# LSH attention and two dense layers on one core: k and q of a head prepared in one joint tile, with SBUF-to-SBUF moves and the bucket rows on GpSimd

## Chip, core and metric

The kernel runs on one core of a Trainium2 chip. The metric is device microseconds of one execution; the time before is the median of three runs, 738.44 us (738.31 to 738.90).

## What is computed

```python
q_bits = (einsum('bhsd,dk->bhsk', q, proj) > 0)      # 6 bits; k_bits alike
mask = q_bucket[:, :, :, None] == k_bucket[:, :, None, :]
scores = where(mask, q @ k.T / 8, -1e9)
attn = softmax(scores);  x = attn @ v                # 2 x 8 heads, 768 tokens, 64 wide
h = max(x @ w1, x @ w2, x @ w3);  y = h @ w_out      # 1536 x 512 -> 768 -> 512
g = where(u >= 1, u, where(u <= -1, 0, (u + 1)**2 / 4))   # u = y @ w_in, 2048 wide
out = g @ w_out2
```

All of it is float32. A product is done on TensorE in the F32R type, each operand split in a high part (rounded to F32R) and a low part (the rest), with the product of the two low parts left out.

## The kernel before

**Attention** works on 16 heads of 768 tokens, each as 6 tiles of 128 queries: 96 tiles. Per tile TensorE makes the scores (`t_qk`, L367 and L368, four matmuls of 384 columns), VectorE takes the row extreme and copies them out of PSUM (`t_max`, L375), ScalarE exponentiates (`t_exp`, L387), TensorE transposes six 128-column blocks (`t_tr`, L395), ScalarE copies the high part out (`t_hi`, L409) and VectorE subtracts the low part (`t_lo`, L413); every three tiles twelve value matmuls follow (`g_pv`, L421), then a correction on ScalarE (`g_corr`) and an addition on VectorE (`g_add`, L440). Every two heads the row sums are inverted, stored to DRAM and loaded back spread over partitions (`pair_*`, L447 to L466), and `norm_*` writes `x_hl` (L475 to L488).

**A head's preparation** runs one to two heads ahead. k and q come from DRAM already transposed, each twice over (rows 0 to 63 and again 64 to 127), in two tiles `kr` and `qr` (`load_one`, L274). GpSimd scales q (L300), makes the high parts `ak` and `aq` of both copies (L293), and subtracts the low parts of 64 rows: of k into `bk` rows 0 to 63, of q into `aq` rows 64 to 127 (`prep_lo`, L318, two halves each). Two SBUF-to-SBUF DMAs copy the high part of q into `bq` rows 0 to 63 and `bk` rows 64 to 127 (`prep_dup`, L305). TensorE multiplies with the split projection (`bits_mm`, L337, three matmuls a half), ScalarE takes the sign (`bits_sign`, L344), and `bits_row` (L354) turns the signs into 12 extra rows at rows 64 to 75, so that the second score matmul (76 rows) adds the mask: the row for `bk` on VectorE, the row for `bq` on GpSimd. Head 0 is prepared ahead of the loop on ScalarE and VectorE.

**The order** of the loop comes from a planner in the program (`Work`, L42 to L94): tasks with an engine, a cost, a due number (in tiles), predecessors and buffers; on each engine it takes, among the tasks that could start within 0.15 us of the earliest, the one due first, and emits them in that order. Every engine and each DMA queue then runs its list strictly in order, with semaphore waits. All DMAs but one are issued on SP. The planner also puts the splitting of the first four weight slices (`w_tick`, `w_steps`, L170 to L203) into the loop.

**The dense layers** (`mlp`, L680 on) follow. Their first matmul blocks (`early`, L732) need batch 0 alone and cover the normalisation of the last two heads, which TensorE would otherwise wait for.

The words that a sentence can't say:

```python
o = s_ps[n % 2][:, half, 0:HALF]
nc.tensor.matmul(out=o, lhsT=hd["aq"][:, qs], rhs=hd["ak"][:, ks], start=True, stop=False)
nc.tensor.matmul(out=o, lhsT=hd["bq"][0:76, qs], rhs=hd["bk"][0:76, ks], start=False, stop=True)
```

Of the kernel before, what the change touches and what calls it, by code (L numbers as in the profile page):

```python
# [41 lines left out]
class Work:  # L42
# [3 lines left out]
    HOP = 0.15  # L46

# [50 lines left out]
def lsh_attention_moe_kernel(  # L98
    ctx: ExitStack,
    tc: tile.TileContext,  # L100
    q: bass.AP,
    k: bass.AP,
# [25 lines left out]
    pj_raw = const.tile([128, 2, 108], F32, name="pj_raw")  # L128
    pj_st = const.tile([128, 3, 108], F32R, name="pj_st")
# [107 lines left out]
    def attention(mlp_steps):  # L237
        with ExitStack() as ax, ExitStack() as sx:
            raw_p = ax.enter_context(tc.tile_pool(name="raw", bufs=1))
# [32 lines left out]
            def load_one(h, side):  # L272
                r = raw_p.tile([128, S], F32, tag=side + "r", name=side + "r")
                nc.sync.dma_start(out=r, in_=(k if side == "k" else q)[h])  # L274
                head.setdefault(h, {})[side + "r"] = r

            def pj_split():
                for i in range(2):
                    nc.scalar.copy(out=pj_st[:, i, :], in_=pj_raw[:, i, :])
                nc.scalar.copy(out=pj_st[0:64, 2, :], in_=pj_raw[0:64, 1, :])  # L280
                for side, i in ((0, 2), (1, 1)):
                    nc.vector.tensor_tensor(
                        out=pj_st[64:128, i, :], in0=pj_raw[64:128, side, :],
                        in1=f32(pj_st[64:128, side, :]), op=ALU.subtract,
                    )

            def prep_hi(h, side, eng, cs=slice(0, S)):
                hd = head[h]
                if "a" + side not in hd:
                    hd["a" + side] = prep_p.tile([128, S], F32R, tag="a" + side, name="a" + side)  # L290
# [596 lines left out]
```

## Time and profile before

| what | value |
|---|---|
| median of three runs | 738.44 us |
| the profiled execution, its own time | 736.59 us |
| its span, first to last instruction | 734.8 us |
| mean granted TensorE clock | 0.993 of full |
| TensorE matmuls busy | 708.8 us (96%) |
| TensorE weight loads busy | 595.7 us (81%) |
| VectorE busy | 553.7 us (75%) |
| ScalarE busy | 405.4 us (55%) |
| GpSimd busy | 348.3 us (47%) |

Busy shares of the whole span mix two parts with different limits, so the stretches have to be read apart. Matmuls are pipelined and the ends of their rows are modelled: starts tell more than lengths. In the rows PE is TensorE's matmuls, PEld its weight loads, DVE VectorE, ACT ScalarE, POOL GpSimd, SP the queue that issues DMAs; Lnn is a line of the kernel before.

### The profile page before, as it was taken

The numbers are of one execution on the slowest core, as the hardware profiler recorded it, in microseconds if no ns is written. First come the engines' busy times: TensorE is split into PE (matmuls) and PEld (weight loads), VectorE is DVE, ScalarE is ACT, GpSimd is POOL, SyncE is SP. The second block draws the span as 40 slices with busy tenths as digits, with TensorE's granted clock in tenths as the row PEclk, the third lists the DMA queues.
The fourth block names the chain that finished last, engine by engine and source line by source line (L and its number), as shares of the span: only waits on it lengthen the run. The fifth ranks groups of instructions, "written<-read, shape, count | busy, mean of one in ns | idle before, by whom it ended". The sixth has DMA issues, their size and how long they took to land.

```text
span 734.8 us, 10243 instructions
## 1 busy us (share of the span) xinstructions
PE 708.8 (96%) x3526; PEld 595.7 (81%) x3526; DVE 553.7 (75%) x898; ACT 405.4 (55%) x789; POOL 348.3 (47%) x338
## 2 busy tenths in 40 slices
PE   8899999999988999999999999999999999999998
PEld 6788888878877888888888888888888888888886
DVE  5899999999999864777544436675687888888854
ACT  5798998988988842333222223467445445444430
POOL 3779689787885301344223312253433443434430
PEclk7999999999999999999999999999999999999999
DMA  4445434534431021222211112112012211112104
GB/s 131 126 119 154 131 85 107 150 98 109 120 110 33 23 65 44 86 87 87 65 50 44 43 58 86 58 58 86 30 58 67 76 57 58 59 57 84 32 0 172
DMA packets 21668, 58.17 MB, mean 79 GB/s; under 512 B 2832, under 2 KB 6000, under 8 KB 21616
## 3 DMA queue, kind: packets, MB, share of 16 engines
q1 hardware_dynamic: 21584, 57.51, 26.2%
q8 instruction: 28, 0.46, 0.2%
q14 instruction: 24, 0.20, 0.1%
q0 software_dynamic: 32, 0.00, 0.0%
HBM read 48.41 MB, written 3.19 MB: 70 GB/s over the span
## 4 chain that ended last, share of the span: by engine, by line
PE 79%; DVE 14%; ACT 2%; issue 2%; DMA 1%; POOL 1%; SPq 0%; ACTq 0%; DVEq 0%
PE b L675 45%; PE b L802 18%; PE u_ps L421 5%; DVE pl L413 5%; PE t_ps L395 5%; DVE p L375 5%; PE s_ps L367 3%; PE s_ps L368 2%; DVE bk L354 2%; DVE u L440 1%; PE pj_ps L337 1%; ACT ph L409 1%; DMA kr<-in_k 1%; ACT z L344 1%; DMA qr<-in_q 1%
## 5 line engine op out<-in xcount | busy, mean ns | idle before, releaser
L675 PE MATMUL b<-x_hl,w 128*128 128x512 f32 (+1 forms) x900 | 202.8, 382 | 0.0
L675 PEld LDWEIGHTS b<-x_hl,w 128*128 128x128 f32 x900 | 164.0, 188 | 33.5
L702 POOL TENSOR_TENSOR g<-r,g 128x512 fp32r<-128x512 f32 x48 | 62.7, 1308 | 125.3 <-ACT g L701 125.3
L802 PE MATMUL b<-w,g 128*128 128x512 f32 (+1 forms) x438 | 108.4, 391 | 0.0
L413 DVE TENSOR_TENSOR pl<-t_ps,ph 128x384 fp32r<-128x384 f32 x192 | 97.9, 550 | 8.1 <-ACT ph L409 6.0
L207 POOL TENSOR_TENSOR w<-wg,w 128x512 fp32r<-128x512 f32 (+1 forms) x42 | 58.9, 1404 | 92.8 <-ACT w L201 80.7
L802 PEld LDWEIGHTS b<-w,g 128*128 128x128 f32 x438 | 81.8, 188 | 18.8
L375 DVE TENSOR_SCALAR_CACHE_REDUCE p<-s_ps 128x768 f32<-128x768 f32 x96 | 90.4, 948 | 7.5 <-PE t_ps L395 4.5
L409 ACT CAST ph<-t_ps 128x384 fp32r<-128x384 f32 x192 | 84.8, 481 | 20.1 <-PE t_ps L395 18.9
L387 ACT ACTIVATE p<-p,nm 128x768 f32<-128x768 f32 x96 | 90.3, 941 | 9.2 <-DVE p L375 8.2
L395 PE MATMUL t_ps<-ident,p 128*128 128x128 f32 x576 | 85.3, 280 | 9.4 <-DVE pl L413 8.8
L180 DVE SCALAR_TENSOR_TENSOR wg<-wg,wr 128x512 f32<-128x512 f32 (+1 forms) x58 | 66.9, 1154 | 34.6 <-ACT wg L178 33.8
L201 ACT CAST w<-wg 128x512 fp32r<-128x512 f32 (+1 forms) x42 | 25.4, 605 | 111.0 <-DVE wg L193 111.0
L395 PEld LDWEIGHTS t_ps<-ident,p 128*128 128x128 f32 x576 | 66.2, 141 | 24.8 <-DVE pl L413 19.2
L675 PE MATMUL b<-x_hl,wx 128*128 128x512 f32 x360 | 86.1, 395 | 0.0
L675 PEld LDWEIGHTS b<-x_hl,wx 128*128 128x128 f32 x360 | 67.8, 188 | 15.8
L367 PE MATMUL s_ps<-ak,aq 128*128 128x384 f32 x192 | 72.1, 375 | 7.9 <-DVE p L375 7.5
L782 DVE SCALAR_TENSOR_TENSOR r<-r,b 128x512 f32<-128x512 f32 x48 | 33.0, 687 | 48.6 <-ACT r L781 48.2
L368 PE MATMUL s_ps<-bk,bq 76*128 76x384 f32 x192 | 67.2, 350 | 0.0
L809 DVE TENSOR_TENSOR acc<-b,acc 128x512 f32<-128x512 f32 (+1 forms) x85 | 56.4, 675 | 8.0 <-PE b L802 8.0
L780 ACT ACTIVATE r<-b,half_sb 128x512 f32<-128x512 f32 x48 | 33.0, 687 | 46.1 <-PE b L675 38.3
L185 DVE TENSOR_SCALAR wg<-wg 128x512 int32<-128x512 int32 (+1 forms) x58 | 53.2, 917 | 2.5
(86 smaller groups left out, 1064.7 us busy)
## 6 DMA issues: line engine op xcount, KB each, us to landing
wr<-in_w SPq DMA_DIRECT2D x50, 512.0 KB, 3.4
kr<-in_k SPq DMA_DIRECT2D x15, 384.0 KB, 3.1
qr<-in_q SPq DMA_DIRECT2D x15, 384.0 KB, 3.1
vr<-in_v SPq DMA_DIRECT2D x16, 192.0 KB, 2.6
rb<-d SPq DMA_DIRECT2D x16, 192.0 KB, 3.9
wr<-in_w SPq DMA_DIRECT2D x8, 384.0 KB, 3.1
bk<-aq SPq DMA_DIRECT2D x15, 192.0 KB, 2.6
bq<-aq SPq DMA_DIRECT2D x15, 192.0 KB, 3.0
```

The costliest lines, as they stand in the source:

```text
L180: nc.vector.scalar_tensor_tensor(out=f32(g), in0=f32(g), scalar=TINY_SQ, in1=f32(high), op0=ALU.is_ge, op1=ALU.mult)
L207: nc.gpsimd.tensor_tensor(out=w[:, 1, 0:cols], in0=f32(g2), in1=f32(w[:, 0, 0:cols]), op=ALU.subtract)
L367: nc.tensor.matmul(out=o, lhsT=hd["aq"][:, qs], rhs=hd["ak"][:, ks], start=True, stop=False)
L368: nc.tensor.matmul(out=o, lhsT=hd["bq"][0:76, qs], rhs=hd["bk"][0:76, ks], start=False, stop=True)
L375: nc.vector.tensor_scalar(out=p.rearrange("p (a k) -> p a k", a=2), in0=s_ps[n % 2][:, :, 0:HALF], scalar1=MASKED, scalar2=MASKED, op0=ALU ...
L387: nc.scalar.activation(out=p, in_=p, func=ACTF.Exp, scale=-1.0, bias=tl[n]["nm"], accum_out=pair[h // 2]["sums"][:, c:c + 1],)
L395: nc.tensor.transpose(out=t_ps[half][:, j * 128:(j + 1) * 128], in_=tl[n]["p"][:, kt * 128:(kt + 1) * 128], identity=ident,)
L409: nc.scalar.copy(out=hi, in_=src)
L413: nc.vector.tensor_tensor(out=lo, in0=src, in1=f32(hi), op=ALU.subtract)
L675: nc.tensor.matmul(out=outp, lhsT=w_[a], rhs=x_[b_], start=(i == 0 and jj == 0), stop=(i == n - 1 and jj == 2),)
L702: nc.gpsimd.tensor_tensor(out=dst[:, 1, cs], in0=src, in1=f32(dst[:, 0, cs]), op=ALU.subtract)
L802: nc.tensor.matmul(out=pb[:, cs], lhsT=gs[f][:, a, tsl], rhs=wt[:, b_, cs], start=(n == 0), stop=(n == len(terms) - 1),)
```

## The change

k and q of a head come in one array `kq` and one tile `r`: k in rows 0 to 63, q in 64 to 127. GpSimd scales the q half, makes one high part `hi` and one low part `lo` (two halves of 384 columns, 128 rows). Five SBUF-to-SBUF DMAs then lay out the operands of the scores: the high part of q to `qa` and `qb` rows 0 to 63, the low part of q to `qa` rows 64 to 127, and, once the bit matmuls have read them, the high part of k over the low part of q in `lo` (`kh`) and the k bit row over q's in `hi` (`kb`). The bit rows of both sides are made by one GpSimd instruction a half over rows 64 to 108 of `qb` (`bits_rows`). The first score matmul is `qa` with `lo`, the second `qb` with `hi`. The projection tile is split in one copy and one subtraction.

Beside that: two raw tiles in place of one of each side; the planner's patience is 0.3 us on ScalarE and VectorE, several costs are changed, the bit tasks of a head are due four tiles earlier, the first two weight slices are loaded at the loop's start; and two of the eight early blocks of the dense layers move behind the others, with one buffer less for their sums.

```diff
-                    task = min((k for t, k in ready if t <= first + 0.15), key=lambda k: k["due"])
+                    task = min((k for t, k in ready if t <= first + self.PATIENCE[eng]), key=lambda k: k["due"])
...
+    PATIENCE = dict(PE=0.15, ACT=0.3, DVE=0.3, POOL=0.15, SP=0.15)
...
-            raw_p = ax.enter_context(tc.tile_pool(name="raw", bufs=1))
+            raw_p = ax.enter_context(tc.tile_pool(name="raw", bufs=2))
...
+            def prep_hi(h, copy, cs=slice(0, S)):
                 hd = head[h]
+                if "hi" not in hd:
+                    for x in ("hi", "lo", "qa", "qb"):
+                        hd[x] = prep_p.tile([128, S], F32R, tag=x, name=x)
+                copy(out=hd["hi"][:, cs], in_=hd["r"][:, cs])
+
+            def prep_lo(h, half, eng):
+                hd = head[h]
+                cs = slice(half * HALF, (half + 1) * HALF)
+                eng.tensor_tensor(out=hd["lo"][:, cs], in0=hd["r"][:, cs], in1=f32(hd["hi"][:, cs]), op=ALU.subtract)
+
+            UP, DOWN = slice(0, 64), slice(64, 128)
+            MOVES = dict(
+                qa=("qa", UP, "hi", DOWN), qb=("qb", UP, "hi", DOWN), ql=("qa", DOWN, "lo", DOWN),
+                kh=("lo", DOWN, "hi", UP), kb=("hi", slice(64, 76), "qb", slice(96, 108)),
+            )
...
-                rows = slice(96, 108) if side == "k" else slice(64, 76)
+                rows = slice(64, 108)
                 eng.tensor_scalar(
-                    out=head[h]["b" + side][64:76, cs], in0=z[rows], scalar1=pc_sb[rows, 0:1],
+                    out=head[h]["qb"][rows, cs], in0=z[rows], scalar1=pc_sb[rows, 0:1],
...
-                    nc.tensor.matmul(out=o, lhsT=hd["aq"][:, qs], rhs=hd["ak"][:, ks], start=True, stop=False)
+                    nc.tensor.matmul(out=o, lhsT=hd["qa"][:, qs], rhs=hd["lo"][:, ks], start=True, stop=False)
                     nc.tensor.matmul(
-                        out=o, lhsT=hd["bq"][0:76, qs], rhs=hd["bk"][0:76, ks], start=False, stop=True
+                        out=o, lhsT=hd["qb"][0:76, qs], rhs=hd["hi"][0:76, ks], start=False, stop=True
                     )
...
             for half in range(2):
                 cs = slice(half * HALF, (half + 1) * HALF)
                 prep_scale(0, nc.scalar, cs)
+                prep_hi(0, nc.scalar.copy, cs)
+                prep_lo(0, half, nc.vector)
                 if half == 0:
                     pj_split()
                 bits_mm(0, half, banks0[half])
+                prep_move(0, "qa", nc.vector.tensor_copy, cs)
+                prep_move(0, "ql", nc.vector.tensor_copy, cs)
+                prep_move(0, "qb", nc.gpsimd.tensor_copy, cs)
+                prep_move(0, "kh", nc.gpsimd.tensor_copy, cs)
                 bits_sign(0, half, banks0[half])
+                bits_rows(0, half, nc.vector)
+                prep_move(0, "kb", nc.vector.tensor_copy, cs)
...
+                sc = task("POOL", 0.9, due, prep_scale, h, nc.gpsimd, after=[ld])
+                hi = task("POOL", 0.8, due, prep_hi, h, nc.gpsimd.tensor_copy, after=[sc], takes=[hp], leaves=[rp])
+                lo = [task("POOL", 1.0, due, prep_lo, h, half, nc.gpsimd, after=[hi], leaves=[rp]) for half in range(2)]
+                for x, after in (("qa", [hi]), ("qb", [hi]), ("ql", lo)):
+                    move[x] = task("SP", 0.1, due, prep_move, h, x, after=after, lag=3.0)
...
-                    done.append(task("DVE", 0.35, due + 6, bits_row, h, half, "k", nc.vector, after=[sg], leaves=[zp]))
-                    done.append(task("POOL", 0.93, due + 6, bits_row, h, half, "q", nc.gpsimd, after=[sg], leaves=[zp]))
+                    mms.append(task("PE", 0.52, due + 2, bits_mm, h, half, pj_ps, after=[hi] + lo, takes=[bp]))
+                    rows.append(task("POOL", 0.75, due + 2, bits_rows, h, half, nc.gpsimd, after=[sg, move["qb"]], leaves=[zp]))
+                kh = task("SP", 0.1, due + 2, prep_move, h, "kh", after=mms + [move["ql"]], lag=3.0)
+                kb = task("SP", 0.1, due + 2, prep_move, h, "kb", after=mms + rows + [move["qa"], move["qb"]], lag=2.5)
...
-            step = low = None
+            step = low = task("SP", 0.2, 4, w_load, 2, lag=6.0)
...
-            early = [(0, w, c) for w in range(3) for c in range(2)] + [(1, w, 0) for w in range(2)]
+            early = [(0, w, c) for w in range(3) for c in range(2)]
```

VectorE, in the loop around a head's bit rows, before (pl is the low part of the transposed tile, p the copied scores, u the sum of a value group, bk the tile that gets the k bit row):

```order
L375 TENSOR_SCALAR p,nm<-s_ps_112 128x768
L413 TENSOR_TENSOR pl<-t_ps_114,ph 128x3x128
L413 TENSOR_TENSOR pl<-t_ps_115,ph 128x3x128
L354 TENSOR_SCALAR bk<-z,pc_sb 12x384
L375 TENSOR_SCALAR p,nm<-s_ps_113 128x768
```

The same engine and place now:

```order
L400 TENSOR_TENSOR pl<-t_ps_115,ph 128x3x128
L362 TENSOR_SCALAR p,nm<-s_ps_113 128x768
L362 TENSOR_SCALAR p,nm<-s_ps_112 128x768
L400 TENSOR_TENSOR pl<-t_ps_114,ph 128x3x128
L400 TENSOR_TENSOR pl<-t_ps_115,ph 128x3x128
L425 TENSOR_TENSOR u<-u_ps,corr 64x384
```

The bit row is gone from VectorE; in the loop it has none in any head.

TensorE, from head 2's last bit matmuls to its first score matmul, before (numbers tell buffers apart; ak_292 and aq_332 are head 2's, ak_187 and aq_211 head 1's):

```order
L337 MATMUL pj_ps_85<-bk_293,pj_st_77 108x384
L367 MATMUL s_ps1_113<-ak_187,aq_211 128x384
L368 MATMUL s_ps1_113<-bk_188,bq_212 128x384
L367 MATMUL s_ps1_113<-ak_187,aq_211 128x384
L368 MATMUL s_ps1_113<-bk_188,bq_212 128x384
L395 MATMUL t_ps0_114<-ident_83,p_416 128x128 x3
L395 MATMUL t_ps1_115<-ident_83,p_416 128x128 x3
L367 MATMUL s_ps0_112<-ak_292,aq_332 128x384
```

The same engine now, at head 2's last bit matmuls (hi_270 and lo_271 are head 2's, lo_195, qa_196, hi_194 and qb_197 head 1's):

```order
L382 MATMUL t_ps0_114<-ident_83,p_317 128x128 x3
L382 MATMUL t_ps1_115<-ident_83,p_317 128x128 x3
L324 MATMUL pj_ps_85<-hi_270,pj_st_77 108x384 x2
L324 MATMUL pj_ps_85<-lo_271,pj_st_77 108x384
L354 MATMUL s_ps0_112<-lo_195,qa_196 128x384
L355 MATMUL s_ps0_112<-hi_194,qb_197 128x384
```

Head 2's last bit matmuls stood one tile ahead of its first score matmul; now they stand ahead of head 1's first score matmul, six tiles of scores earlier.

SP, one head's transfers in the middle of the loop, before (rb is the normaliser, d its DRAM copy):

```order
L305 DMA bk_1315<-aq_1361 64x768
L305 DMA bq_1362<-aq_1361 64x768
L466 DMA rb_1382<-d_1345 64x768 x2
L274 DMA kr_1414<-in_k 128x768
L274 DMA qr_1441<-in_q 128x768
L269 DMA vr_1472<-in_v 128x384
```

And now (hi_748 and qb_751 belong to one head, hi_872, lo_873, qa_874 and qb_875 to the next):

```order
L303 DMA lo_749<-hi_748 64x768
L303 DMA qa_874<-hi_872 64x768
L303 DMA qb_875<-hi_872 64x768
L303 DMA qa_874<-lo_873 64x768
L260 DMA r_916<-in_kq 128x768
L303 DMA hi_748<-qb_751 12x768
L445 DMA d_989<-rt_985 12x128
L451 DMA rb_1024<-d_989 64x768 x2
```

Five moves and one load stand where two moves and two loads stood, and one head's last moves lie among the next head's first.

## Rows read from the trace of the kernel before

**Rows 1.** Busy time by stretch: the attention loop (11 to 266 us) and the dense layers (266 to the end). Columns: start and end, length, then busy us (instructions) of each engine, the granted TensorE clock, the DMA engines' busy share and GB/s.

```profile
core 0: us, PE busy (x) PEld busy (x) DVE busy (x) ACT busy (x) POOL busy (x), PEclk, DMA share, GB/s
11.00:266.00 255.00, 235.51 (x1437) 208.88 (x1436) 234.41 (x479) 216.61 (x461) 184.62 (x213) 0.98 0.38 102
266.00:734.80 468.80, 465.57 (x2064) 381.97 (x2062) 314.00 (x404) 182.81 (x317) 162.72 (x120) 1.00 0.20 65
```

**Rows 2.** The same view of the loop's even middle (40 to 200 us), of its best 20 us, and of 200 to 240 us.

```profile
40.00:200.00 160.00, 151.24 (x944) 136.11 (x945) 152.63 (x312) 142.18 (x303) 131.39 (x152) 1.00 0.45 122
180.00:200.00 20.00, 19.39 (x123) 17.63 (x121) 19.60 (x39) 18.74 (x41) 17.55 (x20) 1.00 0.34 96
200.00:240.00 40.00, 35.05 (x213) 30.21 (x212) 37.36 (x77) 33.37 (x70) 25.99 (x29) 1.00 0.28 73
```

**Rows 3.** The timeline of TensorE's matmuls near 106 to 113 us: start, length, engine, line, operation. L367 and L368 are the score matmuls, L395 the transposes, L421 the value matmuls, L337 the bit matmuls, L451 another small transpose.

```profile
105.59 0.33 PE L367 MATMUL s_ps<-ak,aq 128*128 128x384 f32 x1
...
106.30 0.82 PE L395 MATMUL t_ps<-ident,p 128*128 128x128 f32 x6
106.95 0.27 PE L451 MATMUL pj_ps<-ident,sums 128*12 128x128 f32 x1
...
107.96 0.39 PE L337 MATMUL pj_ps<-aq,pj_st 128*108 128x384 f32 x1
...
108.55 0.35 PE L367 MATMUL s_ps<-ak,aq 128*128 128x384 f32 x1
...
111.68 1.31 PE L421 MATMUL u_ps<-pl,vv 128*128 128x384 f32 x6
112.83 0.34 PE L337 MATMUL pj_ps<-aq,pj_st 128*108 128x384 f32 x1
```

**Rows 4.** The waits over the whole span: who waited for whom, us in total, times, the longest.

```profile
PEld t_ps L395 <- DVE pl L413: 19.2, 46, 1.9
PEld s_ps L367 <- DVE p L375: 14.8, 24, 2.2
```

**Rows 5.** The chain of waits from 11 to 266 us, its shares by line as printed.

```profile
by line: PE u_ps L421 14.5%; DVE pl L413 14.0%; PE t_ps L395 13.9%; DVE p L375 13.0%; PE s_ps L367 7.7%; PE s_ps L368 6.7%; issue 5.8%; DVE bk L354 5.4%; DVE u L440 3.3%; PE pj_ps L337 2.7%; ACT ph L409 2.6%; DMA kr<-in_k 2.1%; ACT z L344 1
```

**Rows 6.** VectorE's k bit rows among the groups of instructions by line: busy us, mean ns of one, idle time before.

```profile
L354 DVE TENSOR_SCALAR bk<-z,pc_sb 12x384 fp32r<-12x384 f32 x32 | 20.2, 641 | 1.5 <-ACT z L344 0.4
```

**Rows 7.** From the same view, the preparation of a head on GpSimd (casts, scaling, subtractions, q bit rows) and the sign on ScalarE.

```profile
L293 POOL CAST ak<-kr 128x768 fp32r<-128x768 f32 x15 | 13.0, 868 | 9.6 <-DMA kr<-in_k 9.2
L300 POOL TENSOR_SCALAR qr<-qr 128x768 f32<-128x768 f32 x15 | 12.7, 845 | 6.0 <-DMA qr<-in_q 4.5 <-DVE p L375 1.3
L293 POOL CAST aq<-qr 128x768 fp32r<-128x768 f32 x15 | 12.4, 830 | 1.0
L318 POOL TENSOR_TENSOR aq<-qr,aq 64x384 fp32r<-64x384 f32 x30 | 30.4, 1030 | 0.9
L318 POOL TENSOR_TENSOR bk<-kr,ak 64x384 fp32r<-64x384 f32 x30 | 30.1, 1018 | 0.5
L354 POOL TENSOR_SCALAR bq<-z,pc_sb 12x384 fp32r<-12x384 f32 x30 | 21.4, 714 | 30.7 <-ACT z L344 26.7 <-issue 2.8
L344 ACT ACTIVATE z<-pj_ps,mhalf_sb,pc_sb 44x384 f32<-44x384 f32 x31 | 20.6, 666 | 3.0 <-PE pj_ps L337 1.8
```

**Rows 8.** The two SBUF-to-SBUF moves of a head: their issue on SP (ns min/median/max, first and last start), and the us to landing, first for the tile bk, then for bq.

```profile
L305 SPq DMA_DIRECT2D bk<-aq x15: 467/472/520, 15.1 to 221.6; - x15
DMA to landing us min/median/max: 2.5/2.6/5.0
L305 SPq DMA_DIRECT2D bq<-aq x15: 548/588/760, 15.6 to 222.2; - x15
DMA to landing us min/median/max: 3.0/3.0/4.5
```

**Rows 9.** The timeline of the hand-over from the last head to the dense layers: the store of the row sums and the load that waits for it (SP), the first dense matmuls (TensorE), the maxima over the early blocks (L718) and the last part of x (L488).

```profile
266.18 0.32 SPq L460 DMA_DIRECT2D d<-rt  x1
...
266.76 14.52 PE L675 MATMUL b<-x_hl,w 128*128 128x512 f32 x80
...
268.85 1.08 SPq L466 DMA_DIRECT2D rb<-d  x2
...
273.86 0.69 DVE L718 TENSOR_TENSOR h<-b,h 128x512 f32<-128x512 f32 x1 [0.38 <-PE b L675]
...
276.65 1.01 DVE L488 TENSOR_TENSOR x_hl<-xr,x_hl 128x384 fp32r<-128x384 f32 x2
278.04 0.69 DVE L718 TENSOR_TENSOR h<-b,h 128x512 f32<-128x512 f32 x1 [0.38 <-PE b L675]
279.48 0.42 DVE L718 TENSOR_TENSOR h<-b,h 128x256 f32<-128x256 f32 x1 [0.74 <-PE b L675]
```

**Rows 10.** The timeline of the start: head 0's second sign, the bit rows on VectorE, the first score pass (L375).

```profile
10.06 0.67 ACT L344 ACTIVATE z<-u_ps,mhalf_sb,pc_sb 44x384 f32<-44x384 f32 x1 [1.45 <-PE u_ps L337]
...
10.76 0.48 DVE L354 TENSOR_SCALAR bk<-z,pc_sb 12x384 fp32r<-12x384 f32 x1 [0.43 <-ACT z L344]
...
11.27 0.97 DVE L354 TENSOR_SCALAR bq<-z,pc_sb 12x384 fp32r<-12x384 f32 x1
...
12.27 0.96 DVE L375 TENSOR_SCALAR_CACHE_REDUCE p<-s_ps 128x768 f32<-128x768 f32 x1
```

**Rows 11.** The waits of SP's own DMA queue; L305 issues the moves of a head's scaled q.

```profile
SPq L305 <- POOL aq L293: 79.6, 12, 10.7
```

More of the change, by code (lines that the diff above doesn't have):

```diff
@@ L270, in load_v @@
                 head[h]["vr"] = vr
[L272 to L275, printed above, removed]
             def pj_split():
[L278 to L290, printed above, removed]
-                    hd["b" + side] = prep_p.tile([128, S], F32R, tag="b" + side, name="b" + side)
-                copy = nc.scalar.copy if eng is nc.scalar else eng.tensor_copy
-                copy(out=hd["a" + side][:, cs], in_=hd[side + "r"][:, cs])
+                nc.scalar.copy(out=pj_st[:, 0, :], in_=pj_raw)
+                nc.vector.tensor_tensor(out=pj_st[:, 1, :], in0=pj_raw, in1=f32(pj_st[:, 0, :]), op=ALU.subtract)
             def prep_scale(h, eng, cs=slice(0, S)):
-                r = head[h]["qr"][:, cs]
+                r = head[h]["r"][64:128, cs]
                 if eng is nc.scalar:
@@ L335, in bits_mm @@
                 cs = slice(half * HALF, (half + 1) * HALF)
-                for i, name in enumerate(("aq", "ak", "bk")):
+                for i, (part, name) in enumerate(((0, "hi"), (1, "hi"), (0, "lo"))):
                     nc.tensor.matmul(
-                        out=bank[0:108, 0:HALF], lhsT=pj_st[:, i, :], rhs=hd[name][:, cs],
+                        out=bank[0:108, 0:HALF], lhsT=pj_st[:, part, :], rhs=hd[name][:, cs],
                         start=(i == 0), stop=(i == 2),
@@ L413, in t_lo @@
                 nc.vector.tensor_tensor(out=lo, in0=src, in1=f32(hi), op=ALU.subtract)
-                if half == 1:
-                    tl.pop(n)
             def g_pv(g, first, count):
@@ L536, in head_tasks @@
                 if h > 1:
-                    lk = task("SP", 0.1, due, load_one, h, "k", takes=[kr], lag=4.0)
-                    lq = task("SP", 0.1, due, load_one, h, "q", takes=[qr], lag=4.0)
-                else:
-                    raw_s["kr"].free, raw_s["qr"].free = [], []
-                hk = task("POOL", 0.8, due, prep_hi, h, "k", nc.gpsimd, after=[lk], takes=[kp], leaves=[kr])
-                sq = task("POOL", 1.8, due, prep_scale, h, nc.gpsimd, after=[lq])
-                hq = task("POOL", 0.8, due, prep_hi, h, "q", nc.gpsimd, after=[sq], takes=[qp], leaves=[qr])
@@ new lines, in head_tasks @@
+                mms, rows = [], []
+                for half in range(2):
+                    zp, bp = place("z", 1), place("pj", 1)
+                    mms.append(task("PE", 0.52, due + 2, bits_mm, h, half, pj_ps, after=[hi] + lo, takes=[bp]))
+                    sg = task("ACT", 0.69, due + 2, bits_sign, h, half, pj_ps, after=[mms[-1]], takes=[zp], leaves=[bp])
+                    rows.append(task("POOL", 0.75, due + 2, bits_rows, h, half, nc.gpsimd, after=[sg, move["qb"]], leaves=[zp]))
@@ L712, in l1 @@
                 if (j, c) not in hraw:
[L713 removed]
+                    hraw[j, c] = t_p.tile([128, TCH], F32, tag=f"h{c}", name=f"h{c}", bufs=1)
                 t = hraw[j, c][:, cs]
```

105 lines of the change are left out of this document (36 added, 69 removed).

## The prediction

> **What bounds the kernel now.** I read the stretches first. The kernel has two parts: a loop of 96 attention tiles from 11 to 266 us, and the dense layers from 266 to the end [rows 1]. In the dense part TensorE is busy 465.57 of 468.8 us, and the change edits neither its matmuls nor their number, so the time can only move in the attention loop and at its two ends. In the loop's even middle, 40 to 200 us, VectorE is busy 152.63 of 160 us (95.4%), ScalarE 142.18 (88.9%), GpSimd 131.39 (82%) [rows 2]. TensorE shows 151.24, but its matmul rows overlap, so I rebuild its need from starts [rows 3]: four score matmuls take 106.30 - 105.59 = 0.71 us, six transposes 106.95 - 106.30 = 0.65, six value matmuls 112.83 - 111.68 = 1.15, three bit matmuls 108.55 - 107.96 = 0.59. A head is six tiles and two value groups of twelve: 6 x 0.71 + 6 x 0.65 + 4 x 1.15 + 2 x 0.59 = 13.94 us. What a head takes: 945 weight loads in 160 us, 90 a head (six tiles of 14, plus 6), so 10.5 heads and 15.2 us each. TensorE thus needs 13.9 of 15.2 (91%), ScalarE 142.18 / 10.5 = 13.5, VectorE 152.63 / 10.5 = 14.5. VectorE bounds, with little room behind it. The waits say the same: TensorE's longest ones in the loop are on VectorE (19.2 us before transposes, 14.8 before scores) [rows 4], and in the chain of waits from 11 to 266 the k bit row alone holds 5.4% of 255 us, 13.8 us [rows 5].
>
> **The change part by part.**
> *VectorE.* It loses the k bit row in the loop: 30 of the 32 of 20.2 us; the first two run before it, so 30 x 0.64 = 19.2 us go [rows 6]. That is 2 x 0.64 = 1.28 a head, which leaves VectorE 14.5 - 1.28 = 13.2 us a head. What is late next is TensorE with 13.9, then ScalarE with 13.5, which loses nothing. I let the new bound reach the share that VectorE held, 95.4%: 13.94 / 0.954 = 14.61, so a head falls from 160 / 10.5 = 15.24 to 14.61, by 0.63. Fifteen heads are prepared in the loop: 15 x 0.63 = **9.4 us gained**. From below: nothing, if TensorE's waits on VectorE turn into waits for something else. From above: the whole 19.2.
> *GpSimd.* A head gives up one 768-column cast (0.87) and two of four subtractions (2 x 1.03); the scaling (0.85), the other cast (0.83), two subtractions and two bit rows (0.71 each) stay, now over 64, 128, 128 and 44 partitions [rows 7]. No row here shows 12 against 44 partitions for one operation; bounds are nothing and the full-height row, 0.43 more for a 384-column half of that cast; I take nothing, since the 64-row subtraction of 384 columns costs 1.03 and the 128-row copy of twice the columns 0.87, so height does not set it. GpSimd falls by 2.9 us a head and stays off the path: 0.
> *Moves.* Five SBUF transfers a head stand where two stood, four of 64 rows and one of 12; the loads fall from two to one. A 64-row move lands in 2.6 to 3.0 us, 5.0 at worst [rows 8]; the 6 KB store has landed 2.7 us after its issue (266.18 to 268.85) [rows 9], so I give the 12-row move 3.0. They are issued on SP alone, 0.5 us each, 1.5 us a head more. Queued behind them are the next head's load, the v load and the normaliser's transfers, due one to two heads ahead. The one new wait near the path is the k bit row, which used to be written in place and is now written on GpSimd and then moved: sign 0.67, bit row 0.71, one or two GpSimd operations in front of it (1.0 to 2.1), SP 1.0 with the high part's move ahead, landing 3.0: 6.4 to 7.5 us after the head's last bit matmul. The new order puts that matmul further ahead of the head's first score matmul: counting the listed TensorE work between by the steps above, 6.9 us for head 1, 7.3 for head 15, 7.8 for head 9, 9.0 for 4 and 10, 9.7 for 2, 6 and 12, 15 and more for the others; before, it was 1.5 for head 2 and 3.5 to 8.8 for most (the two TensorE fences show head 2). That is TensorE work without its idle time, so the move is covered: 0, at most about 1 us for each of heads 1 and 15.
> *Start.* Head 0's second sign ends at 10.7 now; then two bit rows, 0.48 and 0.97, hold VectorE until the first score pass at 12.27 [rows 10]. In the change its second scaling waits for the first sign on ScalarE, its raw half arrives earlier (one load of a half in place of two), and after the sign there remain one row and one copy. I take +0.3 us, between -0.5 and +1.
> *Hand-over.* Two early blocks of 12 wide matmuls leave the work that covers the last head's normalisation and run later, so they cost nothing unless TensorE runs dry. A wide and a narrow block take 278.04 - 273.86 = 4.2 us, a wide one two thirds, 2.8, the two 5.6. The six blocks that stay end near 279.4 (the maximum after the sixth starts at 279.48); the last part of x ends at 276.65 + 1.01 = 277.66 [rows 9]. The cover is 1.7 us: 0, and up to 5.6 us of waiting if the normaliser came that much later.
> *Planner.* Costs, due times and a patience of 0.3 us on two engines reorder every engine. No row prices an order; the nearest is the spread of like stretches: 123 matmuls in the best 20 us, 118 on average [rows 2], 4% of 160 us, so 6.8 us either way. I take 0, since VectorE is relieved in either order.
> **Sum**, on the profiled execution: span 734.8 - 9.4 + 0.3 = 725.7; its own time 736.59 becomes 727.5; the median of the runs shown, 738.44, is 1.85 us above the profiled execution, so 738.44 - 9.1 = **729.3 us**.
>
> **The rivals.**
> *A, TensorE has more room than I rebuilt.* Weight loads fill only 136.11 of 160 us, 85% [rows 2], 13.0 us a head; then ScalarE with 142.18 / 10.5 = 13.54 is next, and 13.54 / 0.954 = 14.19 gives 1.05 a head, 15.7 us: 738.44 - 15.7 + 0.3 = **723.0 us**; the floor, with all 19.2, is 719.5. For it: the chain holds 13.8 us of k bit rows. Against: the starts above leave no gap between matmuls and still need 13.9. The Trainium skill (Perfetto Trace Analysis, Identifying the Most-Contended Engine) states that matmul busy share misleads and the weight-load share tells TensorE's headroom; by that rule the sum would be A's. The trace agrees on the first half (rows overlap) and not on the second: a 384-column score matmul steps by 0.71 / 4 = 0.18 us however its weights are loaded.
> *B, the tiles are bound by their own chain of hops* (transposes, copy, subtraction, transposes again through one bank a half): then freed VectorE time stays idle and the time is 738.44 + 0.3 = **738.7**. For it: from 200 to 240 us VectorE is busy 37.36 of 40 and yet TensorE only 35.05 [rows 2]. Against: the chain names the k bit row itself.
> *C, slower: the k bits come late.* SP takes its transfers in order; if the move of one head's k bits sits behind another head's wait, the 6.4 to 7.5 us grow. With one more wait of 3 us, at 10.5, the heads above wait 3.6, 3.2 and 2.7 (1, 15, 9), 1.5 (4 and 10) and 0.8 (2, 6, 12): 14.9 us, which against the 9.1 gives 738.44 + 5.8 = **744.2**. It decides from about 9.8 us, where these waits sum to the gain. For it: SP today waits 79.6 us in 12 waits, up to 10.7, for GpSimd's casts before such moves [rows 11]. Against: these waits stand early in a head's preparation, and the planner counts them.
> *D, the change does not take the row off VectorE*: excluded by the first order fence, which has none.
>
> **How the numbers follow.** Forecast 0.50, A 0.23, B 0.10, C 0.17. A measurement of this kernel tells some 0.2%, 1.5 us, from no change. Faster: forecast and A, 0.73. Same: B, 0.10. Slower: C, 0.17. The forecast's own range is 723 to 735: TensorE busy at 98%, VectorE's best 20 us [rows 2], or at 93%, its share from 200 to 240. The range over all reaches from A's floor, 719.5, over B to 740.5, the near end of C, and leaves out about 0.06 below and 0.12 above.
>
> **What would show it.** Between 40 and 200 us about 10.9 heads in place of 10.5 (near 985 weight loads); VectorE's share there near 90% (13.2 / 14.6), TensorE's weight-load share near 89% (13.0 / 14.6), GpSimd's near 64%; TensorE's waits on VectorE reduced by a third or more; hardly any wait of score matmuls for a DMA; the first dense matmul near 257.7 in place of 266.76, and from there 468 us as before. I am wrong if score matmuls wait for transfers (C), if VectorE's idle time grows with the loop's length unchanged (B), or if the loop ends before 253 (A).

## The result, and the profile after

The changed kernel takes **719.01 us** (median of four runs, 718.48 to 719.14) against 738.60 (738.31 to 738.90) on the same chip: ratio **0.9733 [0.9717, 0.9750]**. The forecast was 729.3, faster, and its range ended at 719.5: the direction was right and the gain, 19.6 us in place of 9.1, lies 0.5 us beyond the range. The profiled execution took 718.48 us, its span 716.7, 18.1 less than before.

Busy time by stretch, after; columns as in [rows 1].

```profile
core 0: us, PE busy (x) PEld busy (x) DVE busy (x) ACT busy (x) POOL busy (x), PEclk, DMA share, GB/s
11.00:248.00 237.00, 229.79 (x1436) 207.46 (x1437) 210.07 (x448) 213.56 (x461) 143.61 (x168) 0.99 0.42 111
40.00:200.00 160.00, 157.25 (x1000) 143.51 (x999) 146.43 (x313) 148.96 (x323) 102.95 (x121) 1.00 0.46 120
200.00:240.00 40.00, 38.65 (x246) 34.50 (x245) 36.27 (x77) 35.08 (x78) 18.12 (x21) 1.00 0.13 35
11.00:40.00 29.00, 26.59 (x154) 23.90 (x155) 21.31 (x46) 23.15 (x49) 22.54 (x28) 0.92 0.69 192
247.00:716.70 469.70, 466.31 (x2067) 382.43 (x2065) 311.52 (x406) 182.88 (x317) 162.92 (x120) 1.00 0.20 65
```

And the loop's first 29 us in the kernel before:

```profile
11.00:40.00 29.00, 25.59 (x137) 22.45 (x135) 22.79 (x45) 20.58 (x43) 20.70 (x25) 0.87 0.40 108
```

The first 9 us of the loop, before and after:

```profile
11.00:20.00 9.00, 8.96 (x34) 7.66 (x33) 6.09 (x12) 4.85 (x10) 7.22 (x9) 0.57 0.46 128
11.00:20.00 9.00, 8.35 (x39) 7.43 (x39) 6.15 (x13) 5.34 (x11) 7.09 (x10) 0.73 0.83 258
```

Weight loads count the work done, 90 a head. From 40 to 200 us there are 999 for 945 [rows 2]: 11.1 heads of 14.4 us, for 10.5 of 15.2. From 200 to 240 there are 245 for 212, from 11 to 40 there are 155 for 135. At some 15 us a head these are 9.0 (54 loads), 5.5 (33) and 3.3 us (20): 17.8 of the 18.2 us by which the first dense matmul is earlier. Half the gain lies in the even middle; the other half lies at the loop's two ends. The prediction's 40 more loads of the middle (985 for 945) are 6.6 of its 9.4 us; for the ends it carried the same gain a head on, 2.8 us, where 8.8 came. Of the 20 loads of the first 29 us, 6 fall in the first 9, where the mean granted clock is 0.73 in place of 0.57: less time at the lower of its two levels (1.2 and 2.4 GHz). Whether the clock or the order comes first there is not shown.

The waits over the whole span, after (who waited for whom, us in total, times, the longest), answering [rows 4]:

```profile
PEld t_ps L382 <- DVE pl L400: 12.3, 46, 1.5
...
PEld s_ps L354 <- DVE p L362: 4.3, 8, 0.9
```

TensorE's two waits on VectorE fall from 34.0 to 16.6 us, and no score matmul of the loop waits for a DMA. The chain of waits from 11 to 248 us, by line, against [rows 5]:

```profile
by line: PE u_ps L406 18.9%; PE t_ps L382 18.2%; DVE pl L400 12.5%; DVE p L362 11.8%; PE s_ps L354 8.4%; PE s_ps L355 7.8%; issue 3.6%; DVE u L425 3.5%; PE pj_ps L324 3.2%; ACT ph L396 2.5%; ACT p L374 2.4%; ACT corr L418 1.6%; DVE wg L189 
```

The k bit row is gone from it, and TensorE's five lines hold 56.5% of it, for 45.5% before. The head's preparation by line (busy us, mean ns of one, idle before), against [rows 6, 7]:

```profile
L291 POOL TENSOR_TENSOR lo<-r,hi 128x384 fp32r<-128x384 f32 x30 | 29.8, 1011 | 1.4
L341 POOL TENSOR_SCALAR qb<-z,pc_sb 44x384 fp32r<-44x384 f32 x30 | 21.6, 722 | 24.6 <-ACT z L331 21.2 <-PE t_ps L382 2.1
```

Twice the partitions cost the subtraction nothing (1011 ns for 1030), nor does 44 in place of 12 cost the row (722 for 714). The moves by tile (KB each, median us from issue to landing), against [rows 8]:

```profile
qa<-hi SPq DMA_DIRECT2D x15, 192.0 KB, 2.5
qb<-hi SPq DMA_DIRECT2D x15, 192.0 KB, 3.0
qa<-lo SPq DMA_DIRECT2D x15, 192.0 KB, 2.8
```

The timeline of the hand-over, after (last attention addition, last parts of x, the sixth early block's maximum), against [rows 9]:

```profile
249.26 0.56 DVE L425 TENSOR_TENSOR u<-u_ps,corr 64x384 f32<-64x384 f32 x1 [1.93 <-ACT corr L418]
...
257.58 1.02 DVE L473 TENSOR_TENSOR x_hl<-xr,x_hl 128x384 fp32r<-128x384 f32 x2
...
261.32 0.42 DVE L697 TENSOR_TENSOR h<-b,h 128x256 f32<-128x256 f32 x1 [0.74 <-PE b L654]
```

x is complete at 258.6, and TensorE is then still in the six blocks that stayed: the cover holds, by 2.7 us. And the first score pass, against [rows 10]:

```profile
12.26 0.96 DVE L362 TENSOR_SCALAR_CACHE_REDUCE p<-s_ps 128x768 f32<-128x768 f32 x1 [0.78 <-PE s_ps L355]
```

### The profile page after: what moved, and what is told of

The parts are those of the page before. It is cut to its first block, busy times and chain, and to the rows that moved or that the text cites. A ratio compares the mean times of both kernels' runs of the same rounds, so it can differ in the third digit from the quotient of the medians.

```text
span 716.7 us, 10215 instructions
## 1 busy us (share of the span) xinstructions
PE 702.7 (98%) x3526; PEld 594.0 (83%) x3526; DVE 526.5 (73%) x865; ACT 400.9 (56%) x785; POOL 310.6 (43%) x297
## 4 chain that ended last, share of the span: by engine, by line
PE 84%; DVE 11%; ACT 3%; issue 1%; POOL 0%; ACTq 0%; DVEq 0%
PE b L654 46%; PE b L781 19%; PE u_ps L406 6%; PE t_ps L382 6%; DVE pl L400 4%; DVE p L362 4%; PE s_ps L354 3%; PE s_ps L355 3%; DVE u L425 1%; PE pj_ps L324 1%; ACT ph L396 1%; ACT p L374 1%; PE u_ps L253 1%; ACT corr L418 1%; DVE wg L189 1%
## 5 line engine op out<-in xcount | busy, mean ns | idle before, releaser
L400 DVE TENSOR_TENSOR pl<-t_ps,ph 128x384 fp32r<-128x384 f32 x192 | 97.7, 550 | 11.7 <-ACT ph L396 10.4
L180 DVE SCALAR_TENSOR_TENSOR wg<-wg,wr 128x512 f32<-128x512 f32 (+1 forms) x58 | 64.0, 1103 | 37.4 <-ACT wg L178 36.7
L382 PEld LDWEIGHTS t_ps<-ident,p 128*128 128x128 f32 x576 | 64.3, 140 | 20.5 <-DVE pl L400 12.3
L354 PE MATMUL s_ps<-lo,qa 128*128 128x384 f32 x192 | 70.4, 367 | 2.6 <-DVE p L362 2.3
L355 PE MATMUL s_ps<-hi,qb 76*128 76x384 f32 x192 | 66.5, 346 | 0.6 <-DVE hi L305 0.6
```

The lines of the kernel that those rows point to most:

```text
L180: nc.vector.scalar_tensor_tensor(out=f32(g), in0=f32(g), scalar=TINY_SQ, in1=f32(high), op0=ALU.is_ge, op1=ALU.mult)
L354: nc.tensor.matmul(out=o, lhsT=hd["qa"][:, qs], rhs=hd["lo"][:, ks], start=True, stop=False)
L355: nc.tensor.matmul(out=o, lhsT=hd["qb"][0:76, qs], rhs=hd["hi"][0:76, ks], start=False, stop=True)
L382: nc.tensor.transpose(out=t_ps[half][:, j * 128:(j + 1) * 128], in_=tl[n]["p"][:, kt * 128:(kt + 1) * 128], identity=ident,)
L400: nc.vector.tensor_tensor(out=lo, in0=src, in1=f32(hi), op=ALU.subtract)
```

## The experiments

Ratios are to the kernel before on the same chip; 0.1% is 0.74 us. The table places them: weight loads in three stretches and the start of the first dense matmul.

| run | us | ratio [95%] | 11-40 | 40-200 | 200-240 | dense from |
|---|---|---|---|---|---|---|
| before | 738.60 | 1 | 135 | 945 | 212 | 266.76 |
| e4 settings only | 731.45 | 0.9904 [0.9883, 0.9926] | 158 | 950 | 211 | 261.08 |
| e14 change, row back, told | 732.77 | 0.9915 [0.9888, 0.9941] | 135 | 961 | 218 | 262.02 |
| e2 change, row back, untold | 736.16 | 0.9974 [0.9954, 0.9995] | 131 | 928 | 213 | 269.17 |
| e1 row off only | 728.66 | 0.9858 [0.9843, 0.9873] | 138 | 983 | 217 | 257.89 |
| e9 row off and settings | 726.24 | 0.9842 [0.9807, 0.9878] | 152 | 970 | 212 | 258.73 |
| e15 the same, GpSimd lightened | 724.33 | 0.9804 [0.9774, 0.9835] | 142 | 982 | 248 | 252.95 |
| e3 change, old settings | 729.42 | 0.9873 [0.9850, 0.9896] | 146 | 938 | 258 | 258.67 |
| e10 change, GpSimd loaded, untold | 726.94 | 0.9838 [0.9797, 0.9878] | 145 | 939 | 242 | 260.23 |
| e13 change, GpSimd loaded, told | 722.29 | 0.9774 [0.9749, 0.9798] | 143 | 988 | 241 | 252.47 |
| e16 change, eight early blocks | 718.98 | 0.9727 [0.9704, 0.9751] | 152 | 998 | 247 | 248.64 |
| the change | 719.01 | 0.9733 [0.9717, 0.9750] | 155 | 999 | 245 | 248.56 |

"Settings" are the planner's patience, costs, due times, the chaining of the two halves' transposes and the early load of two weight slices; "told" means that the planner counts the added work. The traces of e2, e9 and e10 are of executions above their medians (739.08, 728.57 and 730.11 us), so their losses look larger here than in the times.

**e1: the row alone.** The kernel before without the k bit rows of heads 1 to 15, every engine's order otherwise unchanged; the planner still counts each row, at 0.35 us.

```diff
             def bits_row(h, half, side, eng):
+                if h > 0 and side == "k":
+                    return
```

> The kernel before, its order on every engine unchanged, with the 30 k bit rows of VectorE in the loop left out (the mask rows of k then hold other data). Theory 1, VectorE's time bounds the loop and the whole saving of 18 us comes from freeing it: 738.6 falls to about 720 to 725, the loop ends 14 to 18 us earlier. Theory 2, the freed time is worth little under the old order and the planner's new order brings the rest: 733 to 738.

Measured 728.66 us, 10.5 to 10.7 gained, between the two theories; the prediction's first term was 9.4. Its middle:

```profile
40.00:200.00 160.00, 155.37 (x985) 141.60 (x983) 142.65 (x305) 146.53 (x315) 135.01 (x158) 1.00 0.46 125
```

983 loads, 14.65 us a head: the forecast had 985 and 14.61. The VectorE term was sized rightly.

**e2: the row put back into the change.** Thirty 12x384 rows on VectorE into a tile that nobody reads, behind each bit row; all orders else the same.

```diff
+                if h > 0:
+                    nc.vector.tensor_scalar(
+                        out=extra[64:76, :], in0=z[96:108], scalar1=pc_sb[96:108, 0:1],
+                        scalar2=pc_sb[96:108, 1:2], op0=ALU.mult, op1=ALU.add,
+                    )
...
```

> The changed kernel with 30 bit rows of 12x384 given back to VectorE (written to a tile that nobody reads), every engine's order otherwise unchanged: the reverse of the first run in the new order. Theory 1: 719 rises to 733 to 738. Theory 2: VectorE has idle time in the new order, 719 to 727.

Measured 736.16 us, ten executions from 734.03 to 740.11: the same 19 us of work that e1 took out for 10.5 cost some 17.5 here. Two stretches of its middle:

```profile
124.00:127.00 3.00, 1.09 (x6) 0.62 (x6) 2.94 (x7) 1.54 (x4) 2.87 (x4) 0.94 0.07 12
127.00:135.00 8.00, 7.89 (x35) 7.67 (x36) 5.56 (x13) 5.10 (x11) 0.48 (x1) 0.59 0.24 74
```

VectorE is full from 124 to 127 and TensorE gets 6 matmuls in; behind that its granted clock is 0.59 over 8 us (near the lower of its two levels, 1.2 of 2.4 GHz), and 35 matmuls run there; the 8 us from 152 on, at full clock, hold 55.

**e3 and e4: the settings, each way.** e3 is the change with the settings of before, e4 the kernel before with those of the change (the lines are the diff's).

```diff
-    PATIENCE = dict(PE=0.15, ACT=0.3, DVE=0.3, POOL=0.15, SP=0.15)
+    PATIENCE = dict(PE=0.15, ACT=0.15, DVE=0.15, POOL=0.15, SP=0.15)
...
-            step = low = task("SP", 0.2, 4, w_load, 2, lag=6.0)
+            step = low = None
...
```

> The changed kernel with the planner's old settings: patience 0.15 us on all engines, the old costs of the score pass, the exponential and the sign, bit tasks due four tiles later, the weight load at its old place, transposes of the two halves not chained. Theory 1: 719 to 722. Theory 2: half of the 19.6 us or more is lost, 729 to 735.

> The kernel before with the planner's new settings (patience, costs, due numbers, early weight load, chained transposes), k and q still in two tiles and the k bit row on VectorE. Theory 1: 735 to 740. Theory 2: 728 to 733.

The settings are worth 10.3 us in the change (0.9873 to 0.9733) and 7.1 in the kernel before. In the kernel before they move its first 29 us (158 loads for 135) and leave the middle where it was (950 for 945). e3 comes out where the forecast stood (729.42 for 729.3), but not by its mechanism: its middle has 938 loads, for 985 forecast and 945 before, and its gain lies at the ends. One wait for a DMA stands out in it, in the waits from 60 to 85 us:

```profile
ACT wg L178 <- DMA wr<-in_w: 3.8, 1, 3.8
...
PE t_ps L382 <- DVE pl L400: 3.1, 2, 2.9
```

ScalarE, in its fixed order, stands at a weight slice whose load is late; the copies behind it come late, then VectorE's subtraction, then TensorE's transposes, after a hole of 2.93 us:

```profile
74.69 1.54 PE L382 MATMUL t_ps<-ident,p 128*128 128x128 f32 x6 [2.93 <-DVE pl L400]
75.88 2.25 PE L406 MATMUL u_ps<-ph,vv 128*128 128x384 f32 x6
77.94 1.23 PE L406 MATMUL u_ps<-pl,vv 128*128 128x384 f32 x6
```

Its stretches around it:

```profile
68.00:71.00 3.00, 3.00 (x20) 2.60 (x19) 2.73 (x7) 1.24 (x3) 2.51 (x4) 1.00 0.42 142
71.00:74.50 3.50, 0.76 (x4) 0.44 (x3) 0.43 (x1) 1.49 (x4) 0.88 (x1) 1.00 0.87 248
74.50:78.00 3.50, 3.31 (x13) 3.32 (x14) 2.93 (x7) 3.45 (x8) 0.12 (x1) 0.51 1.06 237
```

After that hole the next 3.5 us run at a granted clock of 0.51, 13 matmuls where 20 had taken 3.0 us before it.

**e5 to e8: one setting each back to the old, in the change.**

```diff
-            step = low = task("SP", 0.2, 4, w_load, 2, lag=6.0)
+            step = low = None
```

> The changed kernel with only the early load of the first two weight slices put back to its old place (issued when the first slice's splitting starts). In the run with all old planner settings ScalarE stood 3.8 us before the first square, until that load landed, TensorE stood 2.9 us and then ran at half clock. Theory 2a, this stall is half of what the planner's settings are worth: 722 to 726 (719 plus 3 to 7). Theory 2b, the order of the tasks is what counts: 719 to 720.

```diff
-    PATIENCE = dict(PE=0.15, ACT=0.3, DVE=0.3, POOL=0.15, SP=0.15)
+    PATIENCE = dict(PE=0.15, ACT=0.15, DVE=0.15, POOL=0.15, SP=0.15)
```

> The changed kernel with only the patience of ScalarE and VectorE back at 0.15 us. Theory 2a: 719 to 721. Theory 2b: 722 to 728.

```diff
-                    mms.append(task("PE", 0.52, due + 2, bits_mm, h, half, pj_ps, after=[hi] + lo, takes=[bp]))
+                    mms.append(task("PE", 0.52, due + 6, bits_mm, h, half, pj_ps, after=[hi] + lo, takes=[bp]))
...
```

> The changed kernel with only the due numbers of the bit tasks and of the two late moves back at four tiles later, so that the k bits come later before the head's first score matmul. Rival C of the prediction (late k bits) would give score matmuls that wait for transfers, 724 to 735; without it 719 to 722.

```diff
-                mx = task("DVE", 0.97, n, t_max, n, after=[qk], takes=[pp], leaves=[sp])
+                mx = task("DVE", 1.05, n, t_max, n, after=[qk], takes=[pp], leaves=[sp])
...
```

> The changed kernel with only the planner's old costs of the score pass, the exponential and the sign, and the transposes of the two halves not chained. Theory 2a: 719 to 721. Theory 2b: 722 to 728, since VectorE's score pass is then planned 8% too long.

Measured e5 725.42 (0.9805 [0.9790, 0.9820]), e6 723.72 (0.9774 [0.9757, 0.9792]), e7 722.01 (0.9756 [0.9742, 0.9771]), e8 726.81 (0.9823 [0.9806, 0.9839]): 5.3, 3.0, 1.7 and 6.6 us, 16.6 together for a joint 10.3. They overlap, and none is the cause alone; that each undoes an order that fits as a whole is a reading, not shown. (e8 undoes the chaining of the transposes too.) e5's is the late weight load again (ScalarE waits 5.5 us for it once). In e8 one score wait of 2.0 us is for the k bits' move: the prediction's case C, once.

**e9: row off and settings, in the old layout** (e1 and e4 together).

> The kernel before with both: the planner's new settings, and the 30 k bit rows of VectorE left out (the mask rows of k then hold other data); k and q still in two tiles, GpSimd still at 82%. Theory 1+2, the row and the planner together are the whole gain and the joint tile matters only as the place where the row can go: 719 to 723. Theory 3, the relief of GpSimd and the loads is part of it: 725 to 731, no better than one of the two alone.

Measured 726.24 us, 0.9842, hardly below e1's 0.9858, and the intervals overlap. Row and settings as they stand here do not make the change; from 200 to 240 us it is where before was (212 loads, at a granted clock of 0.96). But e9's planner still counts the rows that are left out, at 0.35 us each, and what row and settings give when it is told of that was not run by itself.

**e10 and e13: GpSimd's old load put back into the change**, untold and told.

```diff
                 copy(out=hd["hi"][:, cs], in_=hd["r"][:, cs])
+                if h > 0:
+                    copy(out=extra, in_=hd["r"])
...
+                if h > 0:
+                    eng.tensor_tensor(out=extra[0:64, cs], in0=hd["r"][0:64, cs], in1=f32(hd["hi"][0:64, cs]), op=ALU.subtract)
```

and, in e13 alone:

```diff
-                hi = task("POOL", 0.8, due, prep_hi, h, nc.gpsimd.tensor_copy, after=[sc], takes=[hp], leaves=[rp])
-                lo = [task("POOL", 1.0, due, prep_lo, h, half, nc.gpsimd, after=[hi], leaves=[rp]) for half in range(2)]
+                hi = task("POOL", 1.6, due, prep_hi, h, nc.gpsimd.tensor_copy, after=[sc], takes=[hp], leaves=[rp])
+                lo = [task("POOL", 2.0, due, prep_lo, h, half, nc.gpsimd, after=[hi], leaves=[rp]) for half in range(2)]
```

> The changed kernel with the GpSimd work that the change took away put back as extra instructions that write to a tile nobody reads: one 768-column cast and two subtractions of 64x384 a head, 2.9 us; all other orders unchanged. Theory 1+2, GpSimd has room: 719 to 721. Theory 3: 724 to 731, with the bit rows late behind the extra work and VectorE's weight steps longer.

> The changed kernel with the same extra GpSimd work as the run before it with added GpSimd work (per head one 768-column cast and two 64-row subtractions into a tile that nobody reads), but now the planner is told of it (the cast's cost 0.8 doubled to 1.6, the subtraction's 1.0 to 2.0), so that it can place the work. Theory L (GpSimd's load itself costs: its operations make a head's operands late whatever the order): about 727 us as with the work untold, ratio 0.984. Rival O (only the untold lateness cost, by a late k bit move and the half clock behind it): within 2 us of the change, 719 to 721, ratio 0.973 to 0.976. Between 722 and 725 both have a part. Under O no wait of a score matmul over 1 us for the bit rows' move between 40 and 200 us and about 995 weight loads there.

Untold it costs 7.8 us, told 3.3 (722.29 against 718.98 for e16 in the same set of runs). GpSimd is busy 80% of the middle in e10 and 84% in e13, so its share alone does not set the loss. What the trace of e10 shows at one place is an operand that comes late. The timeline of e10 (the bit row on GpSimd, its move's issue on SP, the score matmul that needs it, with the idle time before in brackets):

```profile
143.56 0.67 POOL L346 TENSOR_SCALAR qb<-z,pc_sb 44x384 fp32r<-44x384 f32 x1
...
144.26 0.79 SPq L308 DMA_DIRECT2D hi<-qb  x1
...
146.72 0.66 PE L360 MATMUL s_ps<-hi,qb 76*128 76x384 f32 x1 [2.91 <-POOL hi L287]
```

The bracket names the cast of `hi`, which came last by the profile but makes the next head's tile. Of what this matmul reads, the k bit row on its way from `qb` to `hi` is what was still under way: 2.5 us from its issue to the matmul. This is read from the program and the times; the profile does not name the move here, as it does in e8. If it is so, it is case C's mechanism at one head. Stretches of the same run:

```profile
140.00:143.00 3.00, 3.00 (x21) 2.50 (x19) 2.94 (x8) 2.98 (x8) 0.99 (x2) 1.00 0.56 176
143.00:147.00 4.00, 1.00 (x4) 0.50 (x3) 1.86 (x6) 1.23 (x3) 3.75 (x6) 0.87 0.10 16
147.00:152.00 5.00, 5.00 (x20) 4.81 (x20) 1.99 (x4) 1.99 (x5) 4.25 (x5) 0.50 0.79 219
```

The wait of 2.9 us is followed by 5 us at 0.50: 20 matmuls, for 35 at the pace of the stretch from 140 to 143.

**e11 and e12: attempts at a better version.** e11 makes head 0's two signs after the preparation of both halves; e12 sets the planner's costs to the durations of the rows, with a patience of 0.05, 0.2 and 0.25 us on TensorE, ScalarE and VectorE.

```diff
                 prep_move(0, "kh", nc.gpsimd.tensor_copy, cs)
+            for half in range(2):
+                cs = slice(half * HALF, (half + 1) * HALF)
                 bits_sign(0, half, banks0[half])
```

> The changed kernel with head 0's two signs behind the scaling and rounding of both halves, where the kernel before has them. The prediction took 0.3 us of loss for the new start; its trace shows ScalarE scaling the second half at 6.73 us although the data was there. If the loop's start is what waits: 717 to 718. If TensorE's half clock in the first 16 us or the next head's load decides: 719.

> The changed kernel with planner costs taken from rows of the trace (0.43 and 0.51 for the copy and subtraction of half a tile, 0.56 for three value matmuls, 0.56 for the addition) and a patience of 0.05, 0.2 and 0.25 us on TensorE, ScalarE and VectorE. If nearer costs give a better order: 715 to 718. If the order is near what the engines allow: 719 to 723.

Measured e11 719.62 (0.9746 [0.9715, 0.9777]), no gain (in the change the lower clock, 0.50 to 0.55, lies from 10 to 16 us; the first 5 us are at 1.00); e12 724.21 (0.9809 [0.9778, 0.9841]), 5.6 us worse: these costs and this patience together do not make a better order. No version tried beats the change.

**e14: the row put back, told.** As e2, but the rows are tasks of the planner.

```diff
-                    zp, bp = place("z", 1), place("pj", 1)
+                    zp, bp = place("z", 2), place("pj", 1)
...
+                    task("DVE", 0.65, due + 2, extra_row, h, half, after=[sg], leaves=[zp])
...
```

> The changed kernel with two extra 12x384 rows a head on VectorE into a tile that nobody reads, as in the run with the untold rows, but as tasks of the planner at a cost of 0.65 us, due with the bit rows. The untold rows cost 17.5 us. Theory O (the same 19 us of work costs more when the order does not know of it): the rows cost what removing them from the old order gave, 9 to 11 us: 728 to 731, ratio 0.986 to 0.989. Rival L (with TensorE at 97% of its need any VectorE work costs nearly its own length, told or not): 734 to 738, ratio 0.994 to 0.999. Under O the slices between 40 and 200 us all hold a granted clock of 1.00 or nearly.

Measured 732.77 us, 13.8 above e16 in the same set: between the two theories. Its middle and its end:

```profile
40.00:200.00 160.00, 152.97 (x962) 137.55 (x961) 152.08 (x317) 143.31 (x308) 100.97 (x117) 1.00 0.43 114
200.00:240.00 40.00, 35.63 (x220) 31.24 (x218) 38.11 (x79) 33.81 (x75) 17.54 (x20) 1.00 0.23 64
```

VectorE is back at 152.08 of 160 us, as before the change (152.63 [rows 2]), at full clock throughout, and TensorE back at 961 loads. With the row, VectorE is again the busiest engine beside TensorE, and settings and layout together give 6.3 us (0.9915), about what the settings gave alone (7.1, e4).

**e15: e9 with GpSimd lightened.** k's cast and subtractions are left out from head 2 on; moves from a tile of head 1's k fill the operands, and one load a head goes. The planner is told: the left-out row counts 0 in place of 0.35 us, q's scaling 0.9 in place of 1.8.

```diff
+                if h > 1 and side == "k":
+                    nc.sync.dma_start(out=f32(hd["ak"]), in_=f32(head["kx"]))
+                    return
...
```

> The kernel before with the new planner's settings and without k bit rows after head 0 (as in the run that gave 726.2), and now also without k's work on GpSimd from head 2 on: the cast of k and its two subtractions are left out, and two SBUF-to-SBUF moves from a tile with head 1's k fill both tiles instead, so the scores of heads 2 to 15 are of head 1's k, and their mask rows of k hold other data; the planner is told. GpSimd then does per head what it does in the change (2.9 us less), in the old layout of tiles. Theory G (GpSimd's relief is what the old layout lacked): 719 to 722 us, ratio 0.973 to 0.977, some 995 weight loads between 40 and 200 us. Rival J (the joint tile's shorter chain, fewer buffers and moves matter by themselves): no better than 725, ratio 0.981 or above, some 970 weight loads.

Measured 724.33 us, 0.9804, between its two theories: 2.8 us better than e9 by the ratios, whose intervals overlap, and GpSimd's relief, the planner's costs and the loads changed together. 200 to 240 us now has 248 loads, as the change; the first 29 us have 142 and stay behind its 155.

**e16: eight early blocks**, in the change.

```diff
-            early = [(0, w, c) for w in range(3) for c in range(2)]
+            early = [(0, w, c) for w in range(3) for c in range(2)] + [(1, w, 0) for w in range(2)]
```

> The changed kernel with the eight early blocks of the dense layers of the kernel before (the two wide blocks moved back in front, and the second buffer of their sums); the loop is the same. In the changed kernel the sixth block's maximum starts at 261.3 us and the last part of x ends at 258.6, so the six blocks cover the last head's normalisation. Theory (hand-over term is zero): within 0.2% of the change, 717.5 to 720.5 us. Rival (the two blocks were needed as cover, or they held a buffer that cost time): over 1.5 us faster or slower. Expected dense part 468 us after the first dense matmul, as in the change.

Measured 718.98 us: the hand-over term is zero.

## Why the prediction was right, and where it was wrong

**The signs**, forecast and measured, from 40 to 200 us: weight loads 985 and 999, VectorE 90% and 91.5%, weight loads busy 89% and 90%, GpSimd 64% and 64%; TensorE's waits on VectorE reduced by a third or more, and halved. The one that fails is the first dense matmul: 257.7 and 248.56, beyond the 253 that I had named as A's sign.

**VectorE, right.** Without the row VectorE takes 146.43 / 11.1 = 13.2 us a head, as forecast; the row alone is worth 10.5 us (e1) for the 9.4 of the sum, at a head of 14.65 us for 14.61.

**Height, moves, start, hand-over: right as terms of this change.** Height costs nothing (rows above). No wait of the change is for the k bits' move. The first score pass on VectorE starts at 12.26 us (12.27 [rows 10]). The dense part is 468.1 us (468.0), and e16 moves nothing.

**The step that failed: "Planner ... I take 0, since VectorE is relieved in either order."** The settings are worth 10.3 us in the change, outside the +-6.8 that I had bounded by like stretches of the middle [rows 2]. The reason I gave is false: VectorE is relieved in e3 as well (139.58 of 160 us), and its middle still does 938 loads; TensorE waits there for a late weight slice, and in e8 for a late move. That a head of 14.4 to 14.6 us, with a TensorE need of 13.94, has nothing left to absorb a late item is my reading of this. The bound came from the middle alone, and half of the gain lies at the loop's ends, where the middle's gain a head gives 2.8 of 8.8 us. There e1 has 138 and 217 loads, hardly more than before; the change has 155 and 245.

**The second: "GpSimd ... stays off the path: 0."** Putting the load back, told, costs 3.3 us (e13), though GpSimd was idle 18% of the middle before. The 2.8 us of e15 in the old layout agree, but lie within the intervals and hold other changes too. Some of e13's loss lies at the start: 32 loads from 11 to 20 us at a granted clock of 0.57, for 39 at 0.69 in e16. Which operand comes late in e13 is not shown.

**The terms do not add.** With the row in place the settings give 7.1 us (e4), and settings and layout together 6.3 (e14); with the row off they give 1.2 in the old layout (0.9858 to 0.9842, within the intervals, the planner not told of the missing row) and 10.3 in the new. Removing the row gives 10.5 in the old order and costs 13.8 to 17.5 when undone in the new one. Row and settings, each timed alone in the old kernel, sum to 17.6 us, near the 19.6 by luck: the run that has both, e9, gains 11.7. That e3, the change without the settings, meets the forecast is luck of the same kind, since its middle is slower than before.

**The rivals.** A's number, 719.5 as its floor, was met by another way than A's: A wanted heads of 14.19 us throughout, and the middle has 14.4. TensorE stands at 13.94 / 14.4 = 97% of the need rebuilt from starts. Its weight loads are 143.51 / 160 = 90% busy; in the tightest stretch of the table, 200 to 240 us of e3, they are 93% busy, at 258 loads or 13.95 us a head, just that need. The Trainium skill (Perfetto Trace Analysis, Identifying the Most-Contended Engine) reads the weight-load share as TensorE's headroom; the trace agrees only in part, since of the 15% that it showed idle before, 8.5% were there to be had (13.94 of 15.24 us needed). B fell with e1: freed VectorE time is used. C did not happen in the change; at one head it did in e8 (2.0 us) and, as read above, in e10 (2.9 us).

**What stays open.** e15 stands 5.2 us above the change by the ratios (0.9804 to 0.9733). The loads put about 2 us of it into the first 29 us and 3 into the middle; whether the joint tile's shorter chain, its second raw buffer, the planner's costs of its tasks or merely another order does that is not told apart, and no run changes the raw buffers alone. Nor is it shown which placement decides the stretch from 200 to 240 us: with the row off it has 212 to 258 loads, by order.

## What to carry to other kernels

Where engines run fixed lists and the next bound is within a few per cent, price an edit at the loop's ends as well as in its even middle, and give a changed order a term of its own: here it was as large as the edit that it came with. Before calling an idle engine free, ask which of its results another engine waits for, and how late one of them may be. When an edit and an order come together, time each alone and both; the gains need not add.

## What the runs showed of the hardware

Holes of about 3 us in TensorE's work cost more than their length here. In e3 one lasts 2.93 us and the next 3.5 us stand at a granted clock of 0.51, in e10 one lasts 2.91 and the next 5 us stand at 0.50: the lower level, 1.2 GHz. By the steps of [rows 3], six transposes and six value matmuls take 1.80 us; after e3's hole they take 3.25 (74.69 to 77.94). e10's stretch from 147.17 to 152.15 us holds two score matmuls, twelve transposes and six value matmuls, 2.8 us by the same steps. So the slow stretches add an estimated 1.5 and 2.2 us to the holes. In the change no 10 us slice from 20 us to the end of the loop is below 1.00.

GpSimd's subtraction of 384 columns took 1011 ns over 128 rows and 1030 over 64, its bit row 722 ns over 44 rows and 714 over 12.
